# Retention and MLP on one core: q and k transposed by DMA, row halves in separate PSUM banks without drains, and the sum of own and state outputs on VectorE

## The chip, the cores and the metric

One core of a Trainium2 chip. Times are device microseconds (us) of one execution. A kernel's time is the median of its runs. Ratios are computed from the mean time of one kernel's fast runs over that of the other's of the same rounds on the same chip, so a ratio is not quite the ratio of the medians quoted; the brackets are 95% intervals. "Span" is from the first to the last instruction of the profiled execution, about 2 us shorter than its time. Units of work are called full (128 rows of a sequence) and short (the last 64 of 576 rows, every fifth unit).

## The reference, cut to what matters

```python
# q, k, v: (8 batches, 8 heads, 576, 64) f32; w_in (512, 2048), w_out (2048, 512)
scores = scale * np.matmul(q, k.transpose(0, 1, 3, 2))
Dmat = np.where(rel >= 0, gamma[:, None, None] ** rel[None, :, :], 0.0)   # gamma per head
attn = np.matmul(scores * Dmat[None], v)
x = attn.transpose(0, 2, 1, 3).reshape(8 * 576, 512)
h = x @ w_in
out = np.maximum(0.01 * h, h) @ w_out
```

Both kernels work in chunks of 64 rows: the own part (masked scores times v), and a state per head (the sum of k-transposed times v), carried on and multiplied by q. 40 units feed an MLP over 11 groups of tokens; MLP and attention share TensorE.

## The kernel before: the parts that matter

The attention products are 64x64 matmuls on quadrants of the array. In `burst` one unit's transposes, the next one's scores and states and a third one's outputs are interleaved in two phases with a drain between them; both row halves write the same banks. In a burst of the steady part about 0.33 us lie between the phases:

```python
    def burst(tr=None, sc=None, ot=None):
        ...                                       # cut: the lists of products
        def phase(ph):
            a, c = ("tr", "sc"), ("st", "ot")
            diag = [f for kind in (c if ph else a) for f in products(kind, 0)]
            offd = [f for kind in (a if ph else c) for f in products(kind, 1)]
            ...                                   # cut: two of one, two of the other
        phase(0)
        nc.tensor.drain()
        phase(1)
        if tr is not None:
            ...
            nc.scalar.copy(out=kTs[tr][:, :, 0:n], in_=tiles["tr"][:, 1, :, 0:n])
            (nc.vector.tensor_copy if tr < NFIRST else nc.scalar.copy)(
                out=qTs[tr][:, :, 0:n], in_=tiles["tr"][:, 0, :, 0:n])
        if ot is not None:                        # own + state were summed in PSUM
            nc.scalar.copy(out=xT[:, :, t0 : t0 + n], in_=tiles["ot"][:, :, 0:n])
        if sc is not None:
            ...                                   # cut: mask and states on VectorE
```

Ahead of the steady steps is a stretch that I call *wide*: the second MLP product of groups 0 and 1, 16 blocks of four matmuls, with units 4 to 6 between. After it each step does the loads of a later unit, a burst, and the next casts:

```python
    casts(4)                                      # after the loads of units 5 to 8 and w_out
    ...
    wide = g2_wide([(0, 0), (0, 1), (1, 0), (1, 1)])
    burst(tr=4)
    casts(5)
    for m in range(4):
        wide[m]()
    burst(tr=5, sc=4)
    ...                                           # cut: the same with units 5 and 6
    casts(7)
    loads(9, nc.sync)
    run(ends[3], g1[2] + g2_blocks(2))            # the dense region begins
```

## Time and profile before

| | before |
|---|---|
| time, median (range) | 341.24 us (340.83 to 341.37), 3 runs |
| span, granted clock | 339.0 us, 0.999 |
| start to the first wide block | 43.9 us |
| wide stretch | 43.9 to 62.9: 18.9 us |
| dense region (MLP groups 2 and 3, 11 bursts) | 62.9 to 112.0: 49.1 us |
| steady region | 112.0 to the end: 227.0 us |

A stretch ends where the next begins: the wide one with its last matmul, the dense one with the first scores that go with MLP group 4 (in the kernel before, with the burst that holds them). These four lengths add up to the span. How TensorE fills them is shown in the prediction. One window, from the windows of the kernel before, is that of the wide stretch (start and end; length; busy us and instructions of TensorE, its weight loads, VectorE, ScalarE and GpSimd; granted clock; DMA share; GB/s):

```profile
40.00:60.00 20.00, 19.54 (x276) 10.96 (x274) 8.05 (x16) 7.63 (x15) 4.50 (x5) 1.00 0.71 142
```

### The profile page before, as it was taken

The numbers are of one execution on the slowest core, as the hardware profiler recorded it, in microseconds if no ns is written. First come the engines' busy times: TensorE is split into PE (matmuls) and PEld (weight loads), VectorE is DVE, ScalarE is ACT, GpSimd is POOL, SyncE is SP. The second block draws the span as 40 slices with busy tenths as digits, with TensorE's granted clock in tenths as the row PEclk, the third lists the DMA queues.
The fourth block names the chain that finished last, engine by engine and source line by source line (L and its number), as shares of the span: only waits on it lengthen the run. The fifth ranks groups of instructions, "written<-read, shape, count | busy, mean of one in ns | idle before, by whom it ended". The sixth has DMA issues, their size and how long they took to land.

```text
span 339.0 us, 10339 instructions
## 1 busy us (share of the span) xinstructions
PE 308.6 (91%) x4608; PEld 166.4 (49%) x4608; DVE 114.7 (34%) x212; ACT 163.0 (48%) x306; POOL 86.0 (25%) x95
## 2 busy tenths in 40 slices
PE   1448999989998999999999999999999999999995
PEld 1336854565453445445445444544444544445652
DVE  1562035555544232243414432344143321001011
ACT  3244732566587545555546545465365543332220
POOL 8833721043444230222302430222313200000000
PEclk9999999999999999999999999999999999999999
DMA  8999992599999566059807555396170011000111
GB/s 180 214 206 203 225 232 46 169 190 201 197 209 193 116 148 149 33 125 183 163 31 174 126 126 124 81 202 143 49 158 33 35 39 54 31 33 31 64 62 62
DMA packets 98732, 42.69 MB, mean 126 GB/s; under 512 B 88416, under 2 KB 92512, under 8 KB 98688
## 3 DMA queue, kind: packets, MB, share of 16 engines
q1 hardware_dynamic: 92192, 31.33, 40.2%
q0 software_dynamic: 6208, 10.62, 16.2%
q8 instruction: 36, 0.59, 0.8%
q10 hardware_dynamic: 288, 0.08, 0.1%
q14 instruction: 8, 0.07, 0.1%
HBM read 36.78 MB, written 9.44 MB: 136 GB/s over the span
## 4 chain that ended last, share of the span: by engine, by line
PE 83%; ACT 6%; DVE 4%; DMA 3%; issue 3%; POOL 1%; ACTq 0%; POOLq 0%
PE hps L383 33%; PE yps L406 32%; PE tr L160 5%; PE st L185 3%; DMA t<-in_q_dram 3%; PE sc L172 2%; PE ot L198 2%; PE hps L451 2%; PE ot L213 2%; PE yps L451 2%; ACT t L120 1%; ACT xT L258 1%; DVE s L264 1%; ACT kT L250 1%; ACT gt L390 1%
## 5 line engine op out<-in xcount | busy, mean ns | idle before, releaser
L383 PE MATMUL hps<-xT,w_in 128*128 128x512 f16 (+1 forms) x704 | 146.2, 344 | 3.4 <-ACT gt L390 1.8
L390 ACT ACTIVATE gt<-hps 128x512 f16<-128x512 f32 x144 | 85.4, 601 | 100.5 <-PE hps L383 99.8
L406 PE MATMUL yps<-w_out,gt 128*128 128x512 f16 x512 | 128.1, 379 | 0.0
L383 PEld LDWEIGHTS <-w_in 128*128 128x128 f16 x704 | 67.5, 99 | 59.0 <-issue 4.2
L406 PEld LDWEIGHTS <-gt 128*128 128x128 f16 x512 | 49.1, 98 | 56.1
L288 POOL CAST st<-s 128x512 f16<-128x512 f32 x25 | 24.3, 972 | 143.1 <-DVE s L278 79.4
L264 DVE TENSOR_TENSOR s<-sc,cs 128x512 f16<-128x512 f32 (+1 forms) x40 | 27.6, 689 | 87.0 <-PE sc L172 70.1
L416 DVE COPY osb<-yps 128x512 f32<-128x512 f32 x32 | 22.1, 690 | 98.6 <-PE yps L406 98.6
L160 PE MATMUL tr<-ident,t 64*64 64x64 f16 x1152 | 37.8, 200 | 18.5 <-DVE t L123 10.9
L250 ACT COPY kT<-tr 128x512 f16<-128x512 f16 (+1 forms) x40 | 21.7, 543 | 48.9 <-PE tr L160 21.4
L160 PEld LDWEIGHTS <-t 64*64 64x64 f16 x1152 | 28.0, 113 | 34.5 <-DVE t L123 21.0
L123 POOL TENSOR_TENSOR t<-t,cs 128x512 f16<-128x512 f32 (+1 forms) x32 | 33.7, 1060 | 28.7 <-DMA t<-in_v_dram 17.2
L123 DVE TENSOR_TENSOR t<-t,cs 128x512 f16<-128x512 f32 (+1 forms) x48 | 32.2, 682 | 9.9 <-DMA t<-in_q_dram 8.6
L172 PE MATMUL sc<-qT,kT 64*64 64x64 f16 x576 | 25.8, 198 | 0.0
L120 ACT CAST t<-t 128x512 f16<-128x512 f32 (+1 forms) x40 | 25.3, 633 | 0.8 <-DMA t<-in_k_dram 0.8
L198 PE MATMUL ot<-s,t 64*64 64x64 f16 x576 | 24.5, 198 | 0.8
L213 PE MATMUL ot<-qT,st 64*64 64x64 f16 x512 | 23.8, 197 | 0.5 <-ACT st L288 0.3
L185 PE MATMUL st<-t,t 64*64 64x64 f16 x512 | 21.3, 204 | 3.2 <-issue 0.2
L258 ACT CAST xT<-ot 128x512 f16<-128x512 f32 (+1 forms) x40 | 22.3, 557 | 3.4 <-PE ot L213 3.4
L172 PEld LDWEIGHTS <-kT 64*64 64x64 f16 x576 | 18.4, 113 | 1.3 <-issue 1.3
L198 PEld LDWEIGHTS <-t 64*64 64x64 f16 x576 | 17.0, 111 | 2.9 <-issue 2.3
L251 ACT COPY qT<-tr 128x512 f16<-128x512 f16 (+1 forms) x33 | 18.0, 546 | 0.0
(26 smaller groups left out, 125.8 us busy)
## 6 DMA issues: line engine op xcount, KB each, us to landing
out_dram<-osb SPq DMA_DIRECT2D x36, 256.0 KB, 2.1
t<-in_k_dram SPq DMA_DIRECT2D x25, 256.0 KB, 4.6
t<-in_q_dram SPq DMA_DIRECT2D x24, 256.0 KB, 4.9
t<-in_v_dram SPq DMA_DIRECT2D x24, 256.0 KB, 4.7
t<-in_q_dram POOLq DMA_DIRECT2D x8, 256.0 KB, 7.8
t<-in_v_dram POOLq DMA_DIRECT2D x8, 256.0 KB, 8.6
w_in<-in_moe_w_in_dram POOLq DMA_DIRECT2D x4, 512.0 KB, 12.6
w_out<-in_moe_w_out_dram POOLq DMA_DIRECT2D x4, 512.0 KB, 11.2
```

Of the source, the lines that this page charges most:

```text
L120: nc.scalar.copy(out=t[0:n], in_=t32[u, x][0:n])
L123: eng.tensor_tensor(out=t[0:n], in0=t32[u, x][0:n], in1=tab_sb[0:n, w % 2, x // 2, :].unsqueeze(2).to_broadcast([n, H, D]), op=MUL,)
L160: lambda x=x, p=p, j=j, g=g, hd=hd: nc.tensor.transpose(tiles["tr"][half(g), x, p, half(j)], t16[tr, x][half(j), hd, :], ident[half(j), ha ...
L172: lambda p=p, j=j, g=g, hh=hh: nc.tensor.matmul(out=tiles["sc"][half(j), p, hh, :], lhsT=kTs[sc][half(g), p, half(j)], rhs=qTs[sc][half(g) ...
L185: lambda p=p, j=j, g=g, hd=hd: nc.tensor.matmul(out=tiles["st"][half(g), j, p, :], lhsT=t16[sc, 1][half(j), hd, :], rhs=t16[sc, 2][half(j) ...
L198: lambda p=p, j=j, hh=hh: nc.tensor.matmul(out=tiles["ot"][half(hh), p, half(j)], lhsT=t16[ot, 2][half(j), 2 * p + hh, :], rhs=s16s[ot][ha ...
L213: lambda p=p, j=j, g=g, hh=hh, sx=sx: nc.tensor.matmul(out=tiles["ot"][half(hh), p, half(j)], lhsT=sx[half(g), p, :], rhs=qTs[ot][half(g), ...
L258: nc.scalar.copy(out=xT[:, :, t0 : t0 + n], in_=tiles["ot"][:, :, 0:n])
L264: nc.vector.tensor_tensor(out=s16[0:n].rearrange("s p h t -> s (p h) t"), in0=tiles["sc"][0:n].rearrange("s p h t -> s (p h) t"), in1=mask ...
L383: nc.tensor.matmul(out=hps[:, f, :], lhsT=w_in16[:, c, fc * P : (fc + 1) * P], rhs=xT[:, c, t0 : t0 + tok], start=(c == 0), stop=(c == NP ...
L390: nc.scalar.activation(out=g_tiles[g][:, fb * nf : (fb + 1) * nf, :], in_=hps, func=mybir.ActivationFunctionType.Lrelu,)
L406: nc.tensor.matmul(out=y_cur[g, tb], lhsT=g_tiles[g][:, f, tb * P : (tb + 1) * P], rhs=w_out16[:, f, :], start=(f == 0), stop=(f == NF - 1),)
```

## The change

The intent: take all transposes and their PSUM copies off TensorE and ScalarE from unit 4 on, give each row half of the array its own banks and leave out the drain, and add the own and the state part of an output on VectorE. The q cast moves from VectorE to GpSimd, where one tile for q and k feeds one transposing DMA per unit. Cut to its core:

```diff
-        phase(0)
-        nc.tensor.drain()
-        phase(1)
+    def cast_qk(u):
+        ...                                       # k cast on ScalarE, q cast below
+        (nc.vector if u < NEARLY else nc.gpsimd).tensor_tensor(out=t[0:n, 0], ...)
+        if u >= NPE:                              # NPE = 4
+            qkT[u] = a_pool.tile([P, 2, NP, P], F16, name="qkT")
+            nc.sync.dma_start_transpose(
+                out=qkT[u][:, :, :, 0:n].rearrange("p x c t -> p (x c) t"),
+                in_=t[0:n].rearrange("t x h d -> t (x h d)"))
+    def outputs(u):
+        ...                                       # own and far (state) parts, each row
+        ...                                       # half into banks of its own, no drain
+        nc.scalar.copy(out=tmp[:, :, 0:nb, :], in_=own...)
+        for o in range(2):
+            for c in range(2):
+                nc.vector.tensor_tensor(out=xT[half(o), ps, ...], in0=far[...],
+                                        in1=tmp[...], op=ADD)
     def steady(n):
-            if NEARLY < n + 3 < NU:
-                loads(n + 3, nc.sync)
-            burst(tr=n, sc=n - 1, ot=n - 2)
-            casts(n + 1)
+            if n + 4 < NU:
+                loads(n + 4, nc.sync)
+            scores(n)
+            if n > NFIRST:
+                outputs(n - 1)
+            masks(n)
+            states(n)
+            casts(n + 2)
```

(The steady body is cut to its order.) In the wide stretch, too, units 4 to 6 get their transposes by DMA:

```diff
     for u in (7, 8):
         loads(u, nc.gpsimd)
     casts(4)
     blocks(0, 3)
+    casts(5)
     blocks(1, 3)
-    burst(tr=4)
-    casts(5)
+    some(0, 3)                                    # three wide blocks
+    scores(4)
+    masks(4)
```

The whole diff also loads w_in in 16 pieces instead of 4, loads one unit further ahead, and transposes units 0 to 3 by eight full-size matmuls each.

## The prediction

> **What bounds the kernel now.** I began with the busy times and the chain that ended last.
>
> ```profile
> PE 308.6 (91%) x4608; PEld 166.4 (49%) x4608; DVE 114.7 (34%) x212; ACT 163.0 (48%) x306; POOL 86.0 (25%) x95
> ...
> PE 83%; ACT 6%; DVE 4%; DMA 3%; issue 3%; POOL 1%; ACTq 0%; POOLq 0%
> ```
>
> TensorE is busy for 91% of 339.0 us and carries 83% of the chain, so what counts is what occupies its queue. But busy time overlaps for small matmuls, so I read the size of the attention work from the PE timeline, at a burst in the steady part:
>
> ```profile
> 200.85 1.03 PE L383 MATMUL hps<-xT,w_in 128*128 128x512 f16 x4
> 201.72 1.03 PE L406 MATMUL yps<-w_out,gt 128*128 128x512 f16 x4
> 202.67 0.22 PE L160 MATMUL tr<-ident,t 64*64 64x64 f16 x2
> ...
> 202.91 0.20 PE L160 MATMUL tr<-ident,t 64*64 64x64 f16 x2
> ...
> 202.95 0.29 PE L172 MATMUL sc<-qT,kT 64*64 64x64 f16 x4
> 203.31 0.22 PE L198 MATMUL ot<-s,t 64*64 64x64 f16 x2
> ...
> 203.60 0.29 PE L172 MATMUL sc<-qT,kT 64*64 64x64 f16 x4
> 203.82 1.04 PE L383 MATMUL hps<-xT,w_in 128*128 128x512 f16 x4
> ```
>
> A block of four MLP matmuls takes 0.865 us (201.72 minus 200.85 and its neighbours). The block at 201.72 thus ends at about 202.585, the next begins at 203.82: the burst costs 1.24 us; the next one in the same view costs 1.27 (blocks at 210.73 and 212.86). I use 1.25. Its pieces: 0.085 to enter; two phases, each of 0.28 to 0.31 us, at 0.031 to 0.035 us for four matmuls (two pairs); about 0.33 between the phases, which is the drain; and about 0.2 to come out.
>
> The MLP is 288 such blocks, 249 us. No change of attention touches that. To see where the other 90 us lie, I cut the span into stretches:
>
> ```profile
> 0.00:20.00 20.00, 4.90 (x184) 3.98 (x184) 8.84 (x18) 6.38 (x11) 15.85 (x23) 1.00 0.97 198
> ...
> 75.00:100.00 25.00, 22.97 (x576) 12.53 (x566) 13.08 (x24) 15.46 (x32) 11.10 (x12) 1.00 0.95 198
> ...
> 200.00:225.00 25.00, 24.74 (x340) 12.18 (x339) 7.95 (x15) 13.25 (x25) 6.56 (x7) 1.00 0.48 109
> ```
>
> After the window come PE, PEld, DVE, ACT and POOL busy, the clock, the DMA share and GB/s. There are three regimes. Until about 64 us: loading, four units of attention, then MLP groups 0 and 1 with units 4 to 6 between. From 64 to 112 us a dense region: 32 MLP blocks (27.7 us) share the PE with 11 bursts (13.8 us), yet it lasts 48 us; DMA is near full (0.95), DVE at half. From 112 us a steady region, PE full: 224 blocks x 0.865 = 193.8, 24 bursts x 1.25 = 30, and 3.9 from the last matmul (335.1) to the end: 112 + 227.7 = 339.7 against 339.0. The account closes.
>
> [...]
>
> **The change part by part.** *PE, steady.* A full unit had 96 small matmuls in two phases with a drain. Now 64 remain (16 scores, 16 states, 16 own, 16 far), without a drain. In both kernels four successive matmuls use all four quadrants, so I keep 0.033 us for four. A short unit (every fifth) has 8 scores and 16 outputs, hence a mean of (4x64+24)/5 = 56, or 14 fours: 0.46 us. With 0.085 and 0.2 at the ends, 0.75 us. The saving is 0.50 per burst and 24 x 0.50 = 12 us in the steady region, all on the bounding engine.
>
> *ACT.* It loses both copies after the transposes (543 and 546 ns) and trades the cast to xT for a copy of similar length. ACT isn't the bound; this gives nothing by itself.
>
> *DVE and POOL.* The q cast (0.68 us on DVE) goes to POOL (its v cast takes 1.047 us there). POOL gets 0.97 + 2 x 1.05 = 3.1 us per unit. DVE gets four adds per unit; each reads 256 columns, as the state adds do at 415 ns, so 1.66 us. DVE per full unit: 1.66 + mask 0.69 + states 0.83 to 1.25, about 3.4, plus output copies of 0.69. The 24 steady bursts of before lie between 112 and 279 us, 7.0 us apart; less 0.5 that leaves 6.5, so both fit.
>
> *Dense region.* Now a chain through DVE matters. In DVE's order the adds of unit n-1 precede mask and states of unit n. From outputs(n-1) on PE to outputs(n): 0.25 PE, 0.6 ACT copy, 1.66 adds, 0.69 mask, about 1.05 states, 0.97 state cast on POOL, some 0.3 of handovers: 5.5 us; a short unit skips states and has shorter adds, about 3.3. The mean is 5.0 us, against a PE need of 3.2 blocks x 0.865 + 0.75 = 3.5. Before, no adds lay in that chain. DMA also grows: 0.79 MB of loads at the 198 GB/s shown is 4.0 us[...]. The first step has a wait of its own: unit 7's casts come after the last output copies of the wide part, its transpose is queued behind unit 9's loads, and its scores come after one MLP block. I estimate 6 us of idle PE there (1.6 casts, 2 load issues[...], less 0.9 for the block). So 10 steps: 6 + 9 x 5.0 + the last blocks 3 = 54 us where before took 48.
>
> *Early part.* Four units still use PE transposes, but 8 of full size per unit instead of 32, and DVE now casts q before it works on the states. A startup step took 4 to 5 us; from DVE's pieces (0.42+0.68+0.68+1.05+0.68) I get about 3.6. So the first MLP block comes at about 20 us instead of 23.4. The w_in loads, now 16 instead of 4, cost POOL maybe 6 us of issue, but in order of need. Units 4 to 6 lose drains and copies: before, 20 us passed from 44 to 64 for 16 blocks (13.9 us); I expect 17. Together the dense region starts at 57 instead of 64.
>
> *Sum.* 57 + 54 = 111 instead of 112, then 227 - 12 = 215: span 326, and 2 us from span to the run's time as before (340.8 against 339.0), so 328.
>
> **Rivals.** (1) The transposing DMA is the bound. [...] For it: [...]a DMA share of already 0.95 at 75 to 100 us. Against: [...]two steps of prefetch, and a share of only 0.48 in the steady region. (2) The dense region hides its chain better than I think (adds overlap the next blocks, transposes arrive early): then it is PE-bound at 38 us and the time falls to about 314. For it: DVE's busy share was only half there. (3) The steady saving is smaller, since the order (same row half twice in succession) runs slower than 0.033 per four, say 0.06: then the burst is 1.1 us, the steady saving 3.6, and with the dense region even the time is 336.[...]
>
> **Range and chances.** The steady 12 us is the firmest term. The early 7 us and the dense -6 us are uncertain by about 7 each, mostly independently. So 328, and 313 to 341 for eight in ten. Over 2% faster means below 334.4: 0.76. Within 2%: 0.14, from rival 3 or a longer first stall. Slower by over 2%: 0.10, rival 1.
>
> **What would show it.** In the steady region, from the end of an MLP block to the next one across small matmuls: 0.75 us, no gap inside. Adds of about 0.42 us, four per unit. In the chain of waits: PE's output matmuls waiting for the state cast on POOL, or scores waiting for a DMA into qkT, only before about 111 us. The transposing DMAs: 2 to 5 us from issue to landing. First MLP block near 20 us. The prediction fails if scores wait for transposes in the steady region as well, if the burst remains over 1 us, or if the dense region is PE-bound.

The sum stands as it was made: 57 + 54 + 215 = 326 us of span, and 2 more make 328. Passages that no trace here shows are cut from the text, and two terms with them. The 6 us of the first dense step held one for the transfer, so the terms that are left don't add up to it; in the kernel after, the first transpose there took 3.49 us from issue to landing, and the wait was 5.79. A dense step had one for the time that its transpose takes of the DMA engines, which with the 4.0 us of the loads came to much the same as the chain through VectorE; the 5.0 us in the sum follow from that chain alone, (4 x 5.5 + 3.3)/5. The kernel before has no transposing DMA, so these were estimates that its trace does not bear out. For the forecast of 2 to 5 us from issue to landing it has only the other 256 KB transfers on SyncE's queue to compare with: a median of 2.1 us for stores and of 4.6 to 4.9 for loads.

## The result, and the profile after

The kernel after takes 353.24 us (352.47 to 354.1, 4 runs) against 341.31 of before in the same rounds: ratio 1.0352 [1.0318, 1.0386], slower. The predicted 328 was wrong in direction; 353 lies outside the range.

| stretch | before | predicted | after |
|---|---|---|---|
| start to wide | 43.9 | 40 | 41.9 |
| wide | 18.9 | 17 | 33.1 |
| dense | 49.1 | 54 | 62.9 |
| steady | 227.0 | 215 | 212.8 |
| span | 339.0 | 326 | 350.7 |
| mean granted clock | 0.999 | | 0.961 |

The steady region gave what was promised and a little more. The wide stretch and the dense region took 28.0 us more than before, and the early part 2.0 less. From the page of the kernel after, the busy times, the chain that ended last and two groups (busy us, mean ns of one, then idle time before them):

```profile
PE 301.6 (86%) x3544; PEld 155.8 (44%) x3544; DVE 144.3 (41%) x322; ACT 134.4 (38%) x237; POOL 114.7 (33%) x139
...
PE 68%; DMA 13%; POOL 6%; issue 5%; DVE 3%; SPq 2%; ACT 1%; POOLq 0%; ACTq 0%
...
L320 DVE TENSOR_TENSOR xT<-ot,own 64x256 f16<-64x256 f32 (+1 forms) x144 | 50.3, 388 | 91.2 <-ACT own L314 90.7
...
L194 PE MATMUL sc<-qkT 64*64 64x64 f16 x576 | 13.6, 207 | 28.9 <-DMA qkT<-qk 26.6
```

TensorE does less work (302 instead of 309 us), but its part of the chain fell from 83% to 68%. The scores stood idle for 26.6 us because a transposing DMA had not landed. That is more than the whole loss of 11.7 us in the span, since the steady region won 14.2 us back. The windows of the kernel after say where:

```profile
40.00:60.00 20.00, 11.99 (x101) 5.86 (x100) 1.16 (x3) 2.65 (x6) 5.53 (x6) 0.76 0.92 180
...
75.00:100.00 25.00, 14.81 (x255) 10.47 (x255) 10.66 (x25) 8.80 (x16) 6.65 (x7) 0.80 1.17 205
...
200.00:225.00 25.00, 25.00 (x337) 11.93 (x336) 16.08 (x38) 11.76 (x22) 12.27 (x14) 1.00 1.02 169
```

Between 40 and 60 us TensorE is busy for 12 of 20 us, at a clock of 0.76; between 75 and 100 for 15 of 25, at 0.80. From 200 to 225 us it has no gap at all, although the DMA share (1.02) is nearly as high as at 75 to 100 us. So busy DMA engines alone did no harm there. What differs is how far ahead of its use a transpose lands: those of units 7 to 11, in the dense region, landed about 0.05 us before their scores began; units 27, 29 and 30, issued in this window, landed 1.2 to 3.7 us before. That this lead decides is my reading; no run varies it alone.

**The wide stretch.** From the PE timeline of the kernel after (start, length, what, how many; in brackets the idle time before it and its releaser):

```profile
41.87 1.89 PE L481 MATMUL yps<-w_out,gt 128*128 128x512 f16 x8
...
48.53 0.42 PE L194 MATMUL sc<-qkT 64*64 64x64 f16 x8 [3.91 <-DMA qkT<-qk]
...
58.10 0.43 PE L194 MATMUL sc<-qkT 64*64 64x64 f16 x16 [4.10 <-DMA qkT<-qk]
...
58.98 3.60 PE L481 MATMUL hps<-w_out,gt 128*128 128x512 f16 x8
```

Two waits of 4 us for the transposes of units 4 and 5. After the second, eight MLP matmuls take 3.60 us; eight of the same shape had taken 1.89 at 41.87. The wait is paid twice, as idle time and as slow matmuls after it. Finer windows of the kernel after show a granted clock of 0.50 from 46.9 to 53.6 us and from 57.1 to 63.8, and 1.00 between the two; both low stretches begin within a wait (44.6 to 48.5 and 54.0 to 58.1). In the kernel before it was 1.00 from 43.9 to 62.9 us. The factor of 1.9 agrees with that; that the waits bring the low clock on is my reading of this order in time. Why the transposes were late shows the list of DMA issues of the kernel after between 36 and 60 us (what, issuing queue, how many, KB each, median us to landing):

```profile
w_out<-in_moe_w_out_dram POOLq DMA_DIRECT2D x2, 512.0 KB, 12.8
...
t<-in_v_dram POOLq DMA_DIRECT2D x2, 256.0 KB, 12.9
qkT<-qk SPq DMA_TRANSPOSE x2, 16.7
```

The 16.7 us are one transpose, that of unit 5, issued at 41.36 us, against a median of 3.8 us over the whole run. For unit 4, issued at 39.61, the trace has no landing; its scores began 8.9 us later. Both went out while w_out and loads of later units, issued from GpSimd, were still under way. The transpose of unit 6, issued at 63.26 with the loads done, took 3.0 us. Another queue was no way around the backlog: SyncE issued nothing but these two transposes between 37 and 46 us, and still the one of unit 5 took 16.7 us.

In the same stretch TensorE also waited 1.16 us for a mask on VectorE and 1.57 us for a state cast on ScalarE.

**The dense region.** From the timeline of the kernel after, all engines, with most lines left out: one way through a step and its successors:

```profile
116.49 0.32 PE L194 MATMUL sc<-qkT 64*64 64x64 f16 x16 [2.13 <-DVE s L232]
...
117.42 0.58 ACT L314 COPY own<-ot 128x512 f32<-128x512 f32 x1 [2.43 <-PE ot L306]
...
118.04 1.53 DVE L320 TENSOR_TENSOR xT<-ot,own 64x256 f16<-64x256 f32 x4 [1.70 <-ACT own L314]
...
119.60 0.69 DVE L214 TENSOR_TENSOR s<-sc,cs 128x512 f16<-128x512 f32 x1
...
121.12 0.42 DVE L236 TENSOR_TENSOR s<-stmp,cs 128x256 f32<-128x256 f32 x1
...
122.17 1.05 POOL L139 TENSOR_TENSOR qk<-t,cs 128x512 f16<-128x512 f32 x1
...
123.25 1.24 SPq L147 DMA_TRANSPOSE qkT<-qk  x1
...
127.10 0.29 PE L194 MATMUL sc<-qkT 64*64 64x64 f16 x12 [2.74 <-DMA qkT<-qk]
```

Scores and outputs, the copy of the own part, four adds, mask and states (to 121.54), the state cast and the q cast on GpSimd, the transpose, and then the scores of the unit two steps on: 10.6 us for two steps. It is a loop, and the adds and the transpose both lie in it, one behind the other. A shorter loop runs beside it: all units share one tile for the scores, so the next scores also need the states of this unit to be read out of it. Here that was done at 121.54, and the next scores began at 121.76, 5.3 us after those at 116.49; this is close to the chain that the prediction had. The eleven scores from 82.65 to 137.86 are 5.5 us apart on average, of which the last interval (6.05) ends with a longer run of MLP blocks. So the loop of 5.3 us a step nearly accounts for the pace at this place. But a second limit lies close by. In the whole run the packets of the SyncE queue and their share of the 16 DMA engines are, before and after:

```profile
q1 hardware_dynamic: 92192, 31.33, 40.2%
```

```profile
q1 hardware_dynamic: 126112, 39.73, 58.1%
```

That is 0.581 x 350.7 - 0.402 x 339.0 = 67.5 us of all sixteen engines for 36 transposes, 1.9 us each, if the packets of the loads cost the same in both. The same subtraction between two runs below that load in larger packets (e3 with DMA transposes, 45.7% of 337.1 us; e4 without, 28.0% of 341.6) gives 58.4 us, 1.6 each:

```profile
q1 hardware_dynamic: 51296, 39.73, 45.7%
```

```profile
q1 hardware_dynamic: 17376, 31.33, 28.0%
```

With the loads, 0.79 MB x 0.9 (mean of full and short units) at 198 GB/s = 3.6 us, a unit needs about 5.2 to 5.5 us of the DMA engines. This is an estimate from those numbers, and a rough one: packet times overlap, as the share can pass 1 (1.17 at 75 to 100 us). Loop and transfers demand nearly the same.

**The steady region.** From the PE timeline of the kernel after, one burst between two blocks of four MLP matmuls:

```profile
208.65 1.03 PE L436 MATMUL yps<-w_out,gt 128*128 128x512 f16 x4
209.61 0.32 PE L194 MATMUL sc<-qkT 64*64 64x64 f16 x16
...
210.25 1.04 PE L413 MATMUL hps<-xT,w_in 128*128 128x512 f16 x4
```

210.25 - (208.65 + 0.865) = 0.735 us, against 1.24 to 1.27 before. Over the 23 bursts of the steady region that lie between MLP matmuls the mean, found in the same way, is 0.68 against 1.26 us. No wait for a transpose is seen from 137.86 us on.

### The profile page after: what moved, and what is told of

It is laid out like the page before. It is cut to its first block, busy times and chain, and to the rows that moved or that the text cites. A ratio compares the mean times of both kernels' runs of the same rounds, so it can differ in the third digit from the quotient of the medians.

```text
span 350.7 us, 8376 instructions
## 1 busy us (share of the span) xinstructions
PE 301.6 (86%) x3544; PEld 155.8 (44%) x3544; DVE 144.3 (41%) x322; ACT 134.4 (38%) x237; POOL 114.7 (33%) x139
## 3 DMA queue, kind: packets, MB, share of 16 engines
q1 hardware_dynamic: 126112, 39.73, 58.1%
## 4 chain that ended last, share of the span: by engine, by line
PE 68%; DMA 13%; POOL 6%; issue 5%; DVE 3%; SPq 2%; ACT 1%; POOLq 0%; ACTq 0%
PE hps L413 32%; PE yps L436 30%; DMA qkT<-qk 10%; DMA t<-in_q_dram 3%; POOL t L121 2%; PE sc L194 2%; POOL qk L139 2%; POOL v L159 2%; SPq L121 1%; PE ot L306 1%; DVE xT L320 1%; PE ot L296 1%; PE sc L204 1%; SPq L147 1%; DVE osb L490 1%
## 5 line engine op out<-in xcount | busy, mean ns | idle before, releaser
L320 DVE TENSOR_TENSOR xT<-ot,own 64x256 f16<-64x256 f32 (+1 forms) x144 | 50.3, 388 | 91.2 <-ACT own L314 90.7
L242 POOL CAST st<-s 128x512 f16<-128x512 f32 x25 | 15.3, 610 | 129.9 <-DVE s L232 65.9
L139 POOL TENSOR_TENSOR qk<-t,cs 128x512 f16<-128x512 f32 (+1 forms) x32 | 33.3, 1042 | 32.7 <-DMA t<-in_q_dram 32.7
L314 ACT COPY own<-ot 128x512 f32<-128x512 f32 (+1 forms) x36 | 19.4, 538 | 53.6 <-PE ot L306 33.8
L194 PE MATMUL sc<-qkT 64*64 64x64 f16 x576 | 13.6, 207 | 28.9 <-DMA qkT<-qk 26.6
L159 POOL TENSOR_TENSOR v<-t,cs 128x512 f16<-128x512 f32 (+1 forms) x32 | 33.3, 1042 | 0.6 <-PE ot L296 0.6
L138 ACT CAST qk<-t 128x512 f16<-128x512 f32 (+1 forms) x40 | 24.7, 619 | 4.7 <-DMA t<-in_k_dram 4.7
L306 PE MATMUL ot<-qkT,st 64*64 64x64 f16 x456 | 11.8, 197 | 1.6 <-ACT st L242 1.6
L296 PE MATMUL ot<-s,v 64*64 64x64 f16 x512 | 11.6, 196 | 1.2 <-DVE s L214 1.2
L336 POOL DMA_DIRECT2D w_in<-in_moe_w_in_dram x16 | 9.5, 609 | 3.5 <-DMA t<-in_v_dram 1.6
```

Of the source, the lines that this page charges most:

```text
L138: nc.scalar.copy(out=t[0:n, 1], in_=t32[u, 1][0:n])
L139: (nc.vector if u < NEARLY else nc.gpsimd).tensor_tensor(out=t[0:n, 0], in0=t32[u, 0][0:n], in1=tab_sb[0:n, w % 2, 0, :].unsqueeze(2).to_b ...
L159: (nc.vector if u < NEARLY else nc.gpsimd).tensor_tensor(out=t[0:n], in0=t32[u, 2][0:n], in1=tab_sb[0:n, w % 2, 1, :].unsqueeze(2).to_broa ...
L194: nc.tensor.matmul(out=a[half(j), g, 0, p, :], lhsT=qkT[u][half(g), 1, p, half(j)], rhs=qkT[u][half(g), 0, p, half(j)], start=True, stop=T ...
L242: (nc.scalar.copy if u < NEARLY else nc.gpsimd.tensor_copy)(out=st16[u], in_=s32)
L314: nc.scalar.copy(out=tmp[:, :, 0:nb, :], in_=own[:, 0:nb].rearrange("q j p t -> q p j t"))
```

## The experiments

Theory: the wide stretch is lost to transposes behind queued loads; in the dense region the transposing DMA and the adds each set nearly the same pace, so that undoing one alone shows little. Rivals: the adds alone; the load packets alone; the order of loads and transposes on SyncE; the low clock itself. Experiments start from the kernel after unless they say otherwise. Fourteen ran, in four groups on four chips. The table gives the cuts of all that are compared by stretches; "with" lists what was done. Each length comes from one profiled run, and such a run scatters: in e8, which changes nothing before the dense region, the wide stretch took 37.1 us instead of 33.1. A difference of under about 4 us in the wide stretch is therefore not evidence by itself. The steady lengths of kernels with the same steady code lie within 0.9 us.

| run | with | ratio to before | wide | dense | steady |
|---|---|---|---|---|---|
| after | | 1.0352 | 33.1 | 62.9 | 212.8 |
| e7 | PE transposes, units 4–6 | 1.0098 | 25.6 | 63.8 | 213.0 |
| e1 | PE transposes, units 4–16 | 1.0174 | 23.5 | 65.0 | 213.2 |
| e2 | transposes issued before loads | 1.0269 | 33.4 | 60.1 | 212.9 |
| e6 | masks and states before adds | 1.0198 | 32.7 | 61.2 | 212.9 |
| e5 | sums in PSUM, drain, no adds | 1.0487 | 32.9 | 60.5 | 223.8 |
| e3 | loads in 2 KB rows | 0.9936 | 30.4 | 57.2 | 212.9 |
| e11 | e3 and e6 | 0.9663 | 25.5 | 51.1 | 212.9 |
| e9 | e1 and e6 | 0.9735 | 19.7 | 54.3 | 213.2 |
| e10 | e1, no adds up to unit 16 | 0.9819 | 19.7 | 57.3 | 213.7 |
| e13 | e9, one pause less | 0.9593 | 18.4 | 51.6 | 213.2 |

### The wide stretch alone: e7

```diff
-    NPE = 4
+    NPE = 7
+    transposes(4, "h")           # eight 128x128 each, into PSUM tiles of
+    transposes(5, "h")           # the MLP (unit 6: of the outputs)
     some(0, 3)
     ...
+    transposes(6, "ot")
```

> Only units 4, 5 and 6, those between the blocks of the wide part, are transposed on TensorE; all others as in the changed kernel. If the 33 us of the wide part (18.8 before) come from transposes 4 to 6 that land late behind the queued loads, and from the low clock after these waits, the wide part falls to 20 to 26 us and the time to 341 to 346. If the wide part is held up by something else (the adds, loads that come late), it stays above 348.

Measured: 346.04 us, ratio 1.0098 [1.0047, 1.0149]. The wide stretch fell from 33.1 to 25.6 us. The PE timeline of e7:

```profile
47.43 0.31 PE L203 MATMUL sc<-qkT 64*64 64x64 f16 x8
...
50.37 0.32 PE L203 MATMUL sc<-qkT 64*64 64x64 f16 x16
...
55.27 0.40 PE L184 MATMUL ot<-ident,qk 128*128 128x128 f16 x4 [1.57 <-ACT qk L138]
```

The two scores that had waited for 3.91 and 4.10 us no longer wait. Taking the DMA away from three units alone gave 7.5 us of the wide stretch and 2.5 points of the ratio: late transposes are shown as a cause. The dense region stayed as it was. Of the remaining 6.7 us over the old wide stretch, the clock still took a part (0.84 between 40 and 80 us; the first eight wide matmuls took 3.54 us). The last line shows another: TensorE waits 1.57 us for the cast of k of unit 6, which ScalarE does after a state cast that waits for the adds, mask and states of VectorE.

### Transposes by TensorE up to unit 16: e1

```diff
-    NPE = 4
+    NPE = 17                     # otherwise as e7; in step n also
+            if n + 1 < min(NPE, NU):
+                transposes(n + 1, "h")
```

> Units 4 to 16 are transposed on TensorE again (eight 128x128 each, through the PSUM tiles of the MLP), units 17 to 39 by DMA; everything else as in the changed kernel. Theory A (transposes that arrive late through DMA engines that are full between 40 and 132 us stall TensorE[...]): the waits for qkT go, the dense region ends near 115 us as in the kernel before, the steady saving of 13 us stays, about 330 us. Theory B (the chain through the four DVE adds sets the dense step, as predicted): the adds are all still there, so the time stays at 345 or above. Theory C (only the order on SyncE's queue): also about 330, told from A by the next run.

Measured: 346.86 us (345.83 to 348.41), 1.0174 [1.0131, 1.0217]. The waits for transposes are gone, and the dense region did not get shorter (65.0 us). In the list of waits of e1, TensorE now stands for 5.8 us at the second half of its transposes (for the copy of the first) and for 5.0 us for VectorE's masks and states of the unit before, which free the tile of the scores. The windows of e1, its dense region:

```profile
66.00:131.00 65.00, 49.46 (x773) 28.47 (x771) 34.98 (x83) 30.09 (x55) 22.72 (x26) 0.89 0.72 147
```

The DMA share is down to 0.72, and still the pace is no better. My theory of one cause, DMA, would have ended here; by the words of the expectation this run spoke for the adds alone, which e5 refutes.

### Order on SyncE: e2

```diff
-            if n + 4 < NU:
-                loads(n + 4, nc.sync)          # first in the step
             ...
             casts(n + 2)
+            if n + 4 < NU:
+                loads(n + 4, nc.sync)          # now last
```

> In each step the three loads are issued after the transposing DMA instead of before it, and the first two transposes of the dense region before the loads of units 9 and 10. Same bytes. Theory C (a transpose queues behind 0.79 MB of loads on SyncE's queue): 8 us or more gained, at most 345. Theory A (the DMA engines as a whole are full): within 4 us of 353. Theory B: within 4 us of 353.

Measured: 350.28 us, 1.0269 [1.0236, 1.0303]. Under a point of ratio, 2.8 us in the dense region; 20.8 us of waits for transposes remained (26.6 in the kernel after). The order on the queue is a small part.

### Adds behind mask and states: e6

```diff
-            outputs(n - 1)
+            adds = outputs(n - 1)              # its matmuls and the own copy only
             masks(n)
             states(n)
+            adds()
```

> Only the order on VectorE changes: mask and states of unit n before the four adds of unit n-1. Theory B: the score tile and the state cast on POOL are free 2 us earlier in each dense step, so 10 steps give 6 to 15 us, at most 347. Theory A: within 4 us of 353.

Measured: 349.16 us, 1.0198 [1.016, 1.0237]. The adds left both loops (in the wide stretch, too, they were put behind), yet the dense region gained only 1.7 us. The windows of e6 for that region:

```profile
73.00:134.00 61.00, 43.87 (x696) 23.73 (x698) 30.48 (x73) 24.40 (x44) 24.36 (x27) 0.80 1.24 196
```

A DMA share of 1.24: I read this as the transfers setting the pace, 5.3 us a step (81.15 to 133.96 us for ten), within the 5.2 to 5.5 us estimated above; e11 bears it out. The waits for transposes are as long as ever, 26.7 us.

### Both: e9

> Units 4 to 16 transposed on TensorE and mask and states before the adds: both chains out of the dense region at once. Theory D (two nearly equal paths hold each dense step: cast on POOL, SyncE issue and transpose through full DMA engines; and own copy, adds, mask, states, free score tile; taking one away leaves the other): the dense region falls from 65 us (e1) to 52 or less and the time to 326 to 334. If the low clock or TensorE's own work sets it, it stays above 58 us and the time above 340.

The edit is that of e1 together with that of e6. Measured: 331.53 us (331.16 to 333.91), 0.9735 [0.9681, 0.979]. Against the kernel after, e1 gave 1.8 points of the ratio and e6 1.5; together they gave 6.2. The windows of e9:

```profile
62.00:116.00 54.00, 45.48 (x772) 27.07 (x771) 34.24 (x83) 29.95 (x55) 24.32 (x27) 0.94 0.85 178
```

54.3 us, no full DMA, a clock of 0.94 (the expectation was 52 or less). This shows that two limits stood side by side: with one removed, the other holds most of the region's length. In the wide stretch, too, the order matters: 23.5 us in e1 and 19.7 here, where TensorE no longer waits for the cast of k of unit 6 (e1: 1.57 us, and soon after it four matmuls in 1.91 us, 1.03 in e9) and the clock from 40 to 60 us is 1.00. The two lengths alone lie within the scatter; the missing wait, and 19.7 us again in e10, make the case.

### The adds removed instead of moved: e5 and e10

e5 sums own and state parts in PSUM, as the units before 4 do, with DMA transposes and a drain. e10 is e1 with these sums up to unit 16, and adds from 17.

```diff
     def outputs(u):
+        return outputs_acc(u)    # e5; in e10: if u < 17
```

> From unit 4 on own and state outputs are summed in PSUM again, in two phases with a drain between and one ACT cast to xT; the DVE adds and the copy of the own part are gone. Transposes stay on DMA. Theory B (the chain PE outputs, ACT copy, four DVE adds, mask, states, score tile free, next scores sets the dense step, at about 5 us): the dense region falls from 63 us to 55 or less, while each steady burst grows by about 0.3 us (7 us in all), so 350 or less. Theory A (late transposes): the dense region stays within 3 us of 63 and the time rises to 356 or more.

Measured: 359.22 us, 1.0487 [1.0453, 1.0522]. Without any add, the dense region still takes 60.5 us, with 26.2 us of waits for transposes. The adds alone are refuted as the cause.

> Units 4 to 16 as far as possible as in the kernel before: transposed on TensorE, sums in PSUM with a drain, no adds; units 17 to 39 as in the changed kernel. Theory D: the dense region about 50 us, the steady saving of 13 us kept, 327 to 334. If it stays above 340, the dense region is slow for a reason that is in neither transposes nor adds (the step scores(n) with outputs(n-1), the prefetch distance).

Measured: 334.89 us, 0.9819 [0.9774, 0.9865]: as in e9 both limits are off, and the dense region takes 57.3 us, 3.0 more than in e9 and more than the 50 that I expected; what holds it there was not looked into. Its wide stretch is 19.7 us, as in e9: without adds the wait for the cast is gone as well.

### Cheaper load packets: e3, e4 and e11

A row of 512 contiguous values is loaded for every partition, 2 KB packets instead of eight of 256 B. It loads the wrong values, so the results are wrong, while shapes, bytes and schedule stay.

```diff
-            in_=(q, k, v)[x][b, :, P * w : P * w + n, :].rearrange("h t d -> t h d"),
+            in_=(q, k, v)[x][b].rearrange("h t d -> (h t d)").rearrange(
+                "(t c) -> t c", c=H * D)[P * w : P * w + n],
```

> Wrong result on purpose: each q, k, v load reads the same number of bytes as rows of 2 KB instead of 256 B pieces, so that the DMA engines have an eighth of the packets. Theory A: transposes land early, the waits for qkT shrink to a few us, at most 335 us. Theory B: little change, above 347. Theory C: a part, 340 to 347.

> Control, wrong result on purpose: the kernel before with the same 2 KB loads. Its TensorE waits in the dense region are some 7 us and its early part is bound partly by loading, so 328 to 337 us under all theories. If it gained as much as the changed kernel does from wide loads, the full DMA engines would not be what tells the two kernels apart.

> Wrong result on purpose: 2 KB loads (e3) and mask and states before the adds (e6), transposes on DMA. Theory D: with the DMA engines and the adds both out of the way the dense region falls from 57 us (e3) and 60 us (e6) to 50 or less, and the time from 339 to 333 or less. If the transposing path holds even with free engines (cast, issue and landing in a row), it stays at 56 or more.

Measured: e3 339.27 us (one of its four runs slow), 0.9936 [0.9899, 0.9973]; e4, the control on the kernel before, 342.21 us, 1.0029 [0.9983, 1.0076]; e11, e3 with the order of e6, 329.84 us, 0.9663 [0.9624, 0.9702]. Cheap loads are worth nothing in the old kernel (where I had expected 328 to 337) and 4.2 points in the new one: the new one is short of DMA time. Of the 13.6 us that the span of e3 is shorter, 5.7 lie in the dense region, 2.7 in the wide stretch and 5.3 before it. The 339 us fall between the ranges that I had set for the theories (335 and 340). With the adds behind as well it is 6.9 points, the dense region 51.1 us, with every transpose still by DMA. The windows of e11:

```profile
64.00:115.00 51.00, 37.86 (x693) 21.28 (x691) 31.12 (x73) 23.88 (x44) 24.32 (x27) 0.93 1.02 238
```

238 GB/s in place of 191 in the kernel after's dense region. It is not a version to use, since a row of these inputs has only 64 values. e3 alone shortened the dense region by 5.7 us, more than any other single step: it eases the engines (a DMA share of 0.83 in its dense region, 1.10 in the kernel after) and its transposes land sooner (a median of 3.3 us over the run, 3.8 in the kernel after), while e1 puts work on TensorE in their place. What the adds hold of it shows in the 6.1 us more that e11 gave.

### The clock: e8

```diff
+            if n in (7, 8, 9, 12, 13, 14, 15, 16):
+                # six extra 128x512 matmuls ahead of the scores, result unused
```

> Before the scores of eight of the ten dense steps TensorE does six matmuls of 128x512 that nobody reads (8 x 6 x 0.22 = 10 us of work at full clock), where it would otherwise wait. If the low clock after waits is what stretches the dense MLP blocks (0.86 to 1.73 us), the dummies cost nothing or pay: 345 to 354, with a clock near 1.0 between 80 and 135 us. If the clock does not matter, they add a good part of their 10 us: 357 or more.

Measured: 357.17 us (354.89 to 359.27), 1.0429 [1.0366, 1.0493]. The clock from 80 to 120 us is 0.83, as in the kernel after. The dummies, 48 matmuls or about 10 us at full clock (0.865 us for four), lengthened the dense region by 4.8 us, to 67.7, so about half of them filled gaps, but they did not keep the clock up. (The wide stretch, which the edit doesn't touch, was 4 us longer too.) By the words of the expectation, 357 or more, the clock would not matter. But that disproves nothing: 26.1 us of waits for transposes remained, and they come after the dummies of a step. Inconclusive. How much of the dense loss is the clock and how much the waits stays open.

### A version that beats both: e13, and all units by TensorE: e12 and e14

In e9 TensorE transposes k, waits 0.7 us for the copy out (7.2 us in ten waits), then transposes q. e13 does all eight transposes in a row and then both copies. e12 is e9 with every unit transposed by TensorE, e14 is e13 with the same.

```diff
 # e13, in transposes(u), for x in (1, 0): four transposes into both[:, x]; then
-            (nc.scalar.copy if x else nc.vector.tensor_copy)(out=qkT[u][:, x, :, 0:n], ...)
+            if x == 0:
+                for y in (1, 0):
+                    (nc.scalar.copy if y else nc.vector.tensor_copy)(out=qkT[u][:, y, :, 0:n], ...)
```

> As e9, but all units are transposed on TensorE, none by DMA. If taking the transposes off TensorE is worth what I predicted in the steady region (about 0.25 us and more of matmul time per burst, here eight full-size transposes with entry and exit, 0.4 to 0.6 us), this is 8 to 14 us slower than e9. If they hide, within 4 us of e9.

> e9 with the eight transposes of a unit in a row and both copies after them, so that TensorE no longer waits for ACT between k and q (7.2 us of waits in e9). If these waits lie on the path of the dense region: 322 to 328. If the path is on VectorE there, within 2 us of 331.5. In both cases faster than the kernel before.

> e13, but all units transposed on TensorE. The 23 steady units then pay eight full-size transposes (0.4 us for their columns at the rate of the MLP matmuls, plus another change of tiling in and out, 0.3 us by the trace), so 23 x 0.7 = 16 us above e13. If the transposes cost TensorE only the 0.25 us that I took for the small ones of the kernel before, 6 us above e13.

Measured: e12 364.31 us, 1.068 [1.0631, 1.073], spoilt by the 0.67 us pause in 33 units (21.6 us of waits in its list), an artefact of my edit, as e14 shows. e13 326.79 us (325.33 to 328.82, 6 runs), 0.9593 [0.9562, 0.9625]: correct, and the best. e14 345.18 us (340.68 to 346.33; two of its six runs slow), 1.0066 [1.0019, 1.0113].

e14 and e5 together say what the two halves of the change are worth in the steady region. The profile of e14 fell in the slow state (clock 0.985 over the span), but between 118 and 344 us its clock is 1.00, so only that steady region is read from it. PE timeline of e5, then of e14:

```profile
209.21 1.03 PE L439 MATMUL yps<-w_out,gt 128*128 128x512 f16 x4
210.16 0.32 PE L194 MATMUL sc<-qkT 64*64 64x64 f16 x16
...
211.31 1.04 PE L416 MATMUL hps<-xT,w_in 128*128 128x512 f16 x4
```

```profile
182.62 1.03 PE L435 MATMUL hps<-xT,w_in 128*128 128x512 f16 x4
...
183.96 0.62 PE L185 MATMUL hps<-ident,qk 128*128 128x128 f16 x8
...
184.81 1.04 PE L458 MATMUL yps<-w_out,gt 128*128 128x512 f16 x4
```

By the same working as above, in these bursts and, in brackets, in the mean of 23: e5, transposes by DMA but with a drain, 1.235 us (1.13); e14, no drain but transposes by TensorE, 1.325 us (1.24); the kernel after, neither, 0.735 (0.68); before, both, 1.25 (1.26). Taking only the transposes away gives little (3.2 us of e5's steady region against before), since they had been interleaved with other products around a drain that stayed. Taking only the drain away gives nothing either, because eight full transposes on their own cost nearly as much, 0.59 us here. The steady gain needs both halves. The steady region of e14 took 226.7 us, against 213.2 in e13 and 227.0 before. Of these 13.5 us the bursts account for 23 x (1.24 - 0.68) = 12.9. Between the fast runs of the two kernels lie 4.7 points of the ratio, 16 us; the rest is not explained further, as the profile of e14 is a slow one.

## Why the prediction was wrong, point by point

**Right: the steady region.** "0.75 us" per burst and "24 x 0.50 = 12 us" were 0.735 us (0.68 in the mean) and 14.2 us. Rival 3, the slower order of small matmuls, did not come true: the whole burst takes less than assumed. The adds, "1.66 us" a full unit, took 1.53. Rival 1 is refuted for this region: no scores waited for a transpose there, and over the run 256 KB landed in a median of 3.6 us, at least 3.0 (the 22 full units with a landing in the trace).

**Right within 2 us: the early part.** First MLP block at 20.86 us for "about 20 us"; first wide block at 41.9 for 40.

**Wrong, and 16 of the 25 us of the error: the wide stretch.** The step was "Units 4 to 6 lose drains and copies: before, 20 us passed from 44 to 64 for 16 blocks (13.9 us); I expect 17." It took 33.1. It counted what TensorE no longer did and let the transposes be in time, although one of the windows that I showed has a DMA share of 0.97 during the loading. The transposes of units 4 and 5 stood among the weights and the loads for 8.9 and 16.7 us; the waits (3.91 + 4.10 + 0.46 us) and the clock of 0.50 (46.9 to 53.6 and 57.1 to 63.8 us) made most of the stretch. e7 showed it: without those transposes, 25.6 us. With them on TensorE a second part shows, the adds ahead of mask and states on VectorE: 23.5 us in e1, 19.7 in e9 and e10. In the list of what would show it, I had waits for a transpose "only before about 111 us", but the sum had given them 6 us in the first dense step alone. That one came out as 5.79.

**Wrong, and 9 of the 25: the dense region.** The step was "The mean is 5.0 us" and the total "54 us". The run took 62.9: 7.7 to the first scores instead of 6; 5.46 instead of 5.0 for each of nine steps; and 6.05 instead of 3 for the last blocks. The path through VectorE and GpSimd was sized well ("5.5 us" for a full step; 5.3 in the trace), but I let it and the path through the DMA run side by side and took one mean. The trace shows them in series in one loop of two steps (116 to 127 us), with the shared DMA engines as a second limit as near. e1, e6, e5 (one of them off: 60.5 to 65.0 us; 57.2 in e3) and e9, e10, e11, e13 (both off or eased: 51.1 to 57.3) show that they hold the region together. The term for the transpose was shown by no trace; for a full unit (36 transposes count as 32 full ones) it is 1.8 to 2.1 us of the sixteen engines, an estimate from the 58.4 and 67.5 us above.

**The part that no lower sum could have saved.** Even at 54 us the dense region was predicted to lose 5 us. All gain was to come from the steady region, and 14.2 us did. e13 is the change with its two faults mended, and its gain is nearly just this: its steady region is 13.8 us shorter than that of before, its other stretches together 0.9 us.

**What stays open:** the share of the granted clock in the dense loss, what holds the dense region of e10 and e13 above the 49.1 us of before, and how much of the scatter of the wide stretch is chance: the first eight wide matmuls took 3.54 us in e7 and 1.89 in e1, whose instructions there are the same.

## What to carry to other kernels

In these runs moving work from a full engine to DMA gained in the steady region, where the transposes looked at landed 1.2 to 3.7 us ahead of their use; at the start, behind bulk loads, it came later than the work that it replaced, with waits of about 4 us and, around them, a clock of 0.50. When two resources each need about the same time per step, undo them together in an experiment before calling either harmless. Look for loops over two steps: parts that look parallel within a step may follow each other across steps.

## What the traces show of the transposing DMA

- Time to landing: 256 KB landed in 3.0 us at best and in a median of 3.6 us in the kernel after, behind the bulk loads in 16.7.
- Packets: those of 256 B on SyncE's queue took a median of 18 ns of an engine in both kernels, and a mean of 20.4 ns in the kernel before (85,504, all of loads) and 23.3 in the kernel after (118,272, of which 32,768 are those of the transposes).
- Share of the engines: among the loads a full unit takes 1.8 to 2.1 us of all sixteen, by the estimate above.
- Issue: SyncE is busy with one for at least 1.19 us, median 1.26, up to 3.67 us in the kernel after. The next load follows it: one transpose was issued from 79.12 to 80.38 us, the load behind it at 80.47.
